# Moving 51 loads of a transformer block from SyncE's queue to GpSimd's

## The chip, the cores and the metric

The kernel runs on one core of a Trainium2 chip. The metric is the device time of one execution in microseconds (us); lower is better.

## The reference

One block of a diffusion transformer on x of 2048 tokens by 512 channels in bfloat16: six modulation vectors from c, a layer norm with scale and shift, attention in which each token sees eight keys at distances 0, 2, ..., 14 (32 heads of 16), an output projection with a gate, a second layer norm, and a gated feed-forward layer of width 1792.

```python
mod = (silu(c) @ w_mod).reshape(1, 6, 1, -1)
sa, ca, ga, sb, cb, gb = (mod[:, i] for i in range(6))
h = layernorm(x) * (1 + ca) + sa
q, k, v = split(h @ wqkv)                       # 32 heads of 16
idx = pos[:, None] - 2 * arange(8)[None, :]     # negative: masked
attn = softmax(einsum('bhsd,bhswd->bhsw', q, k[idx]) * 0.25)
x = x + ga * (einsum('bhsw,bhswd->bhsd', attn, v[idx]) @ wo)
h = layernorm(x) * (1 + cb) + sb
x = x + gb * ((silu(h @ w1) * (h @ w3)) @ w2)
```

## The kernel before

**Tiles.** The 2048 tokens are 16 tiles T of 128. `LN1` makes groups of tiles for the first layer norm and the projections to q, k and v; `BLOCKS` pairs of tiles for attention; `FFN` groups for the feed-forward layer.

**First layer norm.** For each pair of tiles VectorE takes mean and variance (L532, L533), GpSimd forms the reciprocal root in two small instructions (L537 adds epsilon, L539 takes the power), and VectorE normalizes (L544). TensorE transposes the result for the first tiles (L604), a DMA transpose does for the last four, and ScalarE applies scale and shift.

**Attention.** q and k stay transposed in SBUF. VectorE multiplies them for all eight distances (L706, "pq"), TensorE sums over heads (L716; for the first tile it also adds a mask, L712, that GpSimd makes in L399 and L400), then softmax. V is written to a scratch tensor in DRAM (`v_scratch_dram`) and read back in shifted rows, 768 KB for a tile (the V load, into two buffers `vsh0` and `vsh1` and, once the projection weights are dead, a third, `vshx`). VectorE multiplies by the weights of attention (L783), TensorE sums (L792), ScalarE copies out, a DMA transposes, TensorE multiplies by `wo` (L804), and VectorE adds to x (L808), whose sum gives the second mean.

**Second layer norm.** ScalarE takes squares (L558), GpSimd forms the reciprocal root (L564, L565), VectorE a bias (L566), ScalarE normalizes (L569). The result is transposed and goes to the feed-forward layer: `w1` and `w3` (L820), silu on ScalarE (L826), a product on VectorE (L831), `w2` (L863, L851), a final addition (L879) and the store.

**Loads.** `w1` and `w3` come in four column groups each (`w1_0` to `w3_3`), `w2` in four row groups (`w2_0` to `w2_3`); VectorE multiplies each `w2` group by the gate (L905) before its first use, and `wo` likewise (L896). The late modulation weights are `wm_g0`, `wm_g1` and `wm_s1`; a second load of x brings the rows of each tile in the order in which attention returns them, as four DMAs for four tiles. All DMAs are issued through `Program.dma` (L127).

**Order.** Every operation is recorded as an `Op` with an engine. The list `ORDER`, written out by hand or by a planner, gives one global order of all 1115 operations; `place` (L147) filters it into one queue for each engine, and `synchronize` (L169) finds the semaphore waits. An engine runs its queue strictly in this order, and an instruction that waits holds everything behind it in the same queue. `dma` has an argument `eng`, "sp" where nothing is said: it decides in whose queue the issuing instruction stands. Its waits stand there too:

```python
def section(e, todo=todo, eng=eng):
    for o in todo:
        for d in o.waits:
            e.wait_ge(d.inc[0], d.inc[2])
        ins = o.fn(e)
```

Before the change SyncE issues everything but the load of c: the loads, the stores of V and of the output, and all 32 DMA transposes. GpSimd runs only constants and the reciprocal roots.

Of the kernel before, what the change touches and what calls it, by code (L numbers as in the profile page):

```python
# [12 lines left out]
D = 512  # L13
H = 32
# [5 lines left out]
KT = D // P  # L20
# [219 lines left out]
def bass_adaLN_cond__sliding_local_dilated__glu_gated_swiglu__prompt_kernel(  # L240
    nc, A_x, A_wqkv, A_wo, B_x, B_w1, B_w3, B_w2, c, w_mod, out
):
    ctx = ExitStack()
    with ctx:
        p = Program(nc, ctx)
        _build(p, *[_full_ap(t) for t in (A_x, A_wqkv, A_wo, B_w1, B_w3, B_w2, c, w_mod, out)])
        p.place(ORDER, SLOTS)
        p.synchronize()
        p.emit()
# [11 lines left out]
def c_act(n):  # L261
    return 66 + n * 107 // 128


def c_dve(n):
    return 60 + n * 137 // 128
# [12 lines left out]
def _build(p, A_x, A_wqkv, A_wo, B_w1, B_w3, B_w2, c, w_mod, out):  # L279
# [6 lines left out]
    def sb(shape, dtype, name):  # L286
        return ctx.enter_context(nc.sbuf_tensor("sb_" + name, shape, dtype))
# [4 lines left out]
    w1 = sb([P, KT, F], bf, "w1")  # L292
    w3 = sb([P, KT, F], bf, "w3")
    w2 = sb([P, NF, D], bf, "w2")
# [38 lines left out]
    def at(shape, dtype, name, off):  # L333
        return nc.alloc_sbuf_tensor_at("sb_" + name, shape, dtype, offset=rbase + off)
# [3 lines left out]
    wm_s = [at([P, KT, 1024], bf, f"wm_s{i}", 12288 * i) for i in range(2)]  # L338
    zrow = at([PAD, D], bf, "zrow", 25600)
    thc, c4, c4s = at([KT, P], f32, "thc", 24576), at([KT, P], bf, "c4", 25088), at([KT, P], bf, "c4s", 25344)  # L340
    wm_g = [at([P, KT, 512], bf, f"wm_g{i}", 12288 * i + 8192) for i in range(2)]
# [6 lines left out]
    def bank(v):  # L348
        return PALL[:, v.at * 512:(v.at + 1) * 512]
# [52 lines left out]
    vkpad, vzrow, vvpad = Val("kpad"), Val("zrow"), Val("vpad")  # L402
# [3 lines left out]
    wm_view = w_mod.rearrange("(t p) n -> p t n", p=P)  # L406
    vcT = Val("cT")
    vx = [Val(f"x{T}") for T in range(NT)]
    vsx = [Val(f"sx{T}") for T in range(NT)]
    vwms, vwmg = [Val("wms0"), Val("wms1")], [Val("wmg0"), Val("wmg1")]  # L410
# [10 lines left out]
    for i in range(3):  # L421
        for half in range(2):
            p.dma(wqkv[:, half::2, i * D:(i + 1) * D], wqkv_view[:, half::2, i * D:(i + 1) * D], ("load", 3 + i), (256, 1024),
                  w=[vwq[i][half]])
    for g in range(1, 4):
        p.dma(x_sb[:, 4 * g:4 * g + 4, :], x_view[:, 4 * g:4 * g + 4, :], ("load", 5 + g), (512, 1024), w=vx[4 * g:4 * g + 4])
    late = {}
    late["wmg0"] = p.dma(wm_g[0][:], wm_view[:, :, 1024:1536], ("load", 9), (512, 1024), w=[vwmg[0]])
    vwo = Val("wo")
    for dl in range(4):  # L430
        late[f"wo{dl}"] = p.dma(wo[32 * dl:32 * dl + 32, :, :],
              bass.AP(A_wo.tensor, A_wo.offset + dl * D, [[16 * D, H], [4 * D, KT], [1, D]]), ("load", 10), (256, 1024), part=[vwo])
    p.dma(v_dram[0:PAD, :], zrow[:], ("load", 11), (16, 1024), r=[vzrow] + wm_hold, w=[vvpad], store=True)
    late["wms1"] = p.dma(wm_s[1][:], wm_view[:, :, 1536:2560], ("load", 12), (512, 2048), w=[vwms[1]])
    late["wmg1"] = p.dma(wm_g[1][:], wm_view[:, :, 2560:3072], ("load", 13), (512, 1024), w=[vwmg[1]])
    w1_view = B_w1.rearrange("(t p) n -> p t n", p=P)
    w3_view = B_w3.rearrange("(t p) n -> p t n", p=P)
    NG = 4
    cuts = [0, 4, 8, 11, 14]
    vw1, vw3, vw2 = [[Val(f"{m}_{g}") for g in range(NG)] for m in ("w1", "w3", "w2")]  # L440
    for g in range(NG):
        a, b = cuts[g] * P, cuts[g + 1] * P
        late[f"w1_{g}"] = p.dma(w1[:, :, a:b], w1_view[:, :, a:b], ("load", 14 + 2 * g), (512, 2 * (b - a)), w=[vw1[g]])
        late[f"w3_{g}"] = p.dma(w3[:, :, a:b], w3_view[:, :, a:b], ("load", 15 + 2 * g), (512, 2 * (b - a)), w=[vw3[g]])
    group_of = [next(g for g in range(NG) if fi < cuts[g + 1]) for fi in range(NF)]
    w2_view = B_w2.rearrange("(t p) n -> p t n", p=P)
    for g in range(NG):
        a, b = cuts[g], cuts[g + 1]
        late[f"w2_{g}"] = p.dma(w2[:, a:b, :], w2_view[:, a:b, :], ("load", 22 + g), (128 * (b - a), 1024), w=[vw2[g]])

    vthc, vcs = Val("thc"), Val("cs")
    k = ("mod", 0)
# [3 lines left out]
         r=[vthc, vcT], w=[vc4])  # L456
# [3 lines left out]
         r=[vc4, vident] + wm_hold, w=[vpc])  # L460
# [169 lines left out]
    vq, vk, vv_dram = {}, {}, {}  # L630
# [142 lines left out]
    def values(T, i, val):  # L773

        vv = Val("vsh", vshpool)
        p.dma(lambda: vv.at[:], bass.AP(v_dram, (PAD + T * P - 2) * D, [[4 * D, 32], [-4 * D, 4], [1, 6 * D]]), ("vl", T), (128, 6144),
              r=[vv_dram[T]] + ([] if T % 2 else [vv_dram[T - 1]] if T else [vvpad]), w=[vv], cost=640, again=True)
        vr = Val("pr", pqpool)

        def av(e):  # L780
            a_w = bass.AP(val.at, i * 8 * H, [[2 * 8 * H, P], [H, 8], [0, DH], [1, H]])
            v_w = bass.AP(vv.at, 2 * D, [[6 * D, P], [-2 * D, 2], [D, 4], [1, D]])
            return e.tensor_tensor(bass.AP(vr.at, 0, [[8 * D, P], [1, 8 * D]]), v_w, a_w, ALU.mult)  # L783

        avs[T] = p.op("dve", av, C_PQ, ("av", T), r=[val, vv], w=[vr], lock=True)
        vo, vt = Val("ps_o", psum), Val("ot", otpool)

        def acc(e):
            b = bank(vo)
            for wf in range(2):  # L790
                for c in range(4):
                    ins = e.matmul(b[32 * c:32 * c + 32, :], ind[:], bass.AP(vr.at, (4 * wf + c) * D, [[8 * D, P], [1, D]]),  # L792
                                   start=(wf == 0), stop=(wf == 1), tile_position=(0, 32 * c))
            return ins

        p.op("pe", acc, C_RED, ("ac", T), r=[vr, vind], w=[vo], tiled=True)
        va = Val("oa", oapool)
        p.op("act", lambda e: e.activation(va.at[:], bank(vo), ACT.Copy), c_act(512), ("ac", T), r=[vo], w=[va])
        p.dma(lambda: vt.at[:], lambda: va.at[:], ("ac", T), (128, 1024), r=[va], w=[vt], cost=1250, transpose=True)
        vy = Val("ps_y", psum)  # L800

        def wop(e):
            for ft in range(KT):
                ins = e.matmul(bank(vy), vt.at[:, ft, :], wo[:, ft, :], start=(ft == 0), stop=(ft == KT - 1))  # L804
            return ins

        p.op("pe", wop, 4 * MM, ("wo", T), r=[vt, vsc_wo], w=[vy])
        p.op("dve", lambda e: e.scalar_tensor_tensor(x_sb[:, T, :], bank(vy), 1.0, x_sb[:, T, :], op0=ALU.mult, op1=ALU.add,  # L808
                                                     accum_out=sx[:, T, :]), c_dve(512) + 12, ("rs", T), r=[vy], w=[vx[T], vsx[T]])
# [90 lines left out]
    for g in range(NG):  # L900
# [3 lines left out]
        a, b = cuts[g], cuts[g + 1]  # L904
# [3 lines left out]
    for T in range(0, NT, 4):  # L908
        loads = []
        for c in range(4):  # L910
            p.dma(x_sb[32 * c:32 * c + 32, T:T + 4, :], bass.AP(x2d.tensor, x2d.offset + (T * P + c) * D, [[4 * D, 32], [P * D, 4], [1, D]]),
                  ("xr", T), (128, 1024), part=vx[T:T + 4], group=loads)
    for groups in BLOCKS:
        vls = [logits(Ts) for Ts in groups]
        ves = [shift(Ts, vl) for Ts, vl in zip(groups, vls)]
        for Ts, vl, ve, vx_ in zip(groups, vls, ves, exps(groups, vls, ves)):
            val = softmax(Ts, vl, ve, vx_)
            for i, T in enumerate(Ts):
                values(T, i, val)
# [102 lines left out]
```

## Time and profile before

| | us |
|---|---|
| median of the two runs | 246.49 |
| the two runs | 245.53 and 247.45 |
| the profiled execution | 247.83 |
| its span, first to last instruction | 245.8 |
| TensorE busy | 234.7 (96%) |
| VectorE busy | 173.1 (70%) |
| ScalarE busy | 154.5 (63%) |
| GpSimd busy | 20.9 (8%) |

The span leaves out some 2 us of the execution's own time. A line of the timeline gives the start and the duration of an instruction (or of several in a row), its engine, its line in the kernel and what it writes and reads; in brackets stands the idle time before it and what ended it. "SPq" and "POOLq" are instructions in the queue of SyncE or GpSimd that issue DMAs. PE is TensorE, DVE VectorE, ACT ScalarE, POOL GpSimd.

### The profile page before, as it was taken

The page shows a single profiled execution, that of the slowest core. Times are in us where ns is not written, and L with a number is a line of the kernel's source. Part 1 is how long each engine was busy: PE and PEld are TensorE (multiplying, and loading weights), DVE is VectorE, ACT ScalarE, POOL GpSimd, SP SyncE. Part 2 cuts the span into 40 slices and gives each one's busy share as a digit, 9 for nine tenths or more (in the row PEclk, how much of TensorE's full clock was granted, in tenths as well). Part 3 has the DMA queues.
Part 4 walks back from the last instruction along what each step waited for, and adds up shares of the span by engine and source line. Part 5 has one row for each costly group of instructions (what it writes and reads, how often), then busy time and mean ns, then how long its engine had stood idle before and what let it go on. Part 6 is the DMA issues. An engine that isn't in the chain of part 4 may idle for free.

```text
span 245.8 us, 4285 instructions
## 1 busy us (share of the span) xinstructions
PE 234.7 (96%) x1669; PEld 120.1 (49%) x1669; DVE 173.1 (70%) x305; ACT 154.5 (63%) x305; POOL 20.9 (8%) x52
## 2 busy tenths in 40 slices
PE   7799999999998999899899999999999999999994
PEld 2557555444556666545443434443334444444473
DVE  4567999999897899988999996592942322142621
ACT  2168677797998889764587879456556944351200
POOL 4124111002000200031000001100000110000000
PEclk9799999999999999999999999999999999999999
DMA  6999979879958687703332964443031120010002
GB/s 191 345 311 350 303 273 207 188 185 350 299 131 249 217 214 244 173 21 67 87 126 59 266 164 154 72 109 121 21 87 23 43 65 16 9 57 9 3 19 67
DMA packets 39348, 36.21 MB, mean 147 GB/s; under 512 B 18832, under 2 KB 36256, under 8 KB 39328
## 3 DMA queue, kind: packets, MB, share of 16 engines
q1 hardware_dynamic: 39320, 35.94, 51.6%
q8 instruction: 13, 0.21, 0.4%
q14 instruction: 7, 0.06, 0.1%
q10 hardware_dynamic: 8, 0.00, 0.0%
HBM read 27.53 MB, written 4.21 MB: 129 GB/s over the span
## 4 chain that ended last, share of the span: by engine, by line
PE 48%; DMA 3%; ACT 2%; DVE 0%; issue 0%; DVEq 0%
PE pall L820 30%; PE pall L863 12%; PE pall L804 3%; DMA sb_h<-sb_xn 2%; PE pall L792 2%; DMA out_dram<-sb_o 1%; ACT sb_h L589 1%; PE pall L851 1%; DVE sb_o L879 0%; ACT sb_xn L569 0%; PE pall L716 0%; ACT sb_hh L830 0%; DVEq L225 0%
## 5 line engine op out<-in xcount | busy, mean ns | idle before, releaser
L820 PE MATMUL pall<-sb_h,sb_w 128*128 128x512 bf16 (+1 forms) x560 | 101.5, 337 | 1.4 <-ACT sb_h L589 1.0
L820 PEld LDWEIGHTS pall<-sb_h,sb_w 128*128 128x128 bf16 x560 | 51.5, 98 | 50.4 <-ACT sb_sg L826 5.8
L826 ACT ACTIVATE sb_sg<-pall 128x512 bf16<-128x512 f32 (+1 forms) x70 | 34.0, 514 | 26.5 <-PE pall L820 25.9
L863 PE MATMUL pall<-sb_w,sb_hh 128*128 128x512 bf16 x196 | 43.5, 379 | 0.0
L706 DVE TENSOR_TENSOR sb_pq<-sb_q,sb_kT 128x4096 bf16<-128x4096 bf16 x16 | 36.3, 2282 | 0.0
L656 PE MATMUL pall<-sb_h,sb_wqkv 128*128 128x512 bf16 (+1 forms) x160 | 33.0, 350 | 1.0 <-DVE sb_h L619 0.6
L830 ACT ACTIVATE sb_hh<-pall 128x256 bf16<-128x256 f32 (+1 forms) x56 | 26.3, 493 | 9.6 <-PE pall L820 9.0
L863 PEld LDWEIGHTS pall<-sb_w,sb_hh 128*128 128x128 bf16 x196 | 19.0, 98 | 22.8 <-DVE sb_hh L831 0.3
L783 DVE TENSOR_TENSOR sb_pq<-sb_vsh,sb_al 128x4096 bf16<-128x4096 bf16 x12 | 27.3, 2286 | 1.1 <-PE pall L716 0.8
L831 DVE TENSOR_TENSOR sb_hh<-sb_sg,sb_hh 128x256 bf16<-128x256 bf16 (+1 forms) x56 | 18.5, 352 | 11.7 <-ACT sb_hh L830 11.3
L879 DVE TENSOR_TENSOR sb_o<-pall,sb_x 128x512 bf16<-128x512 f32 (+1 forms) x18 | 11.0, 628 | 16.8 <-PE pall L863 12.4
L656 PEld LDWEIGHTS pall<-sb_h,sb_wqkv 128*128 128x128 bf16 x160 | 15.0, 102 | 15.2 <-ACT sb_v L685 1.2
L834 DVE TENSOR_TENSOR sb_hh<-sb_sg,pall 128x512 bf16<-128x512 bf16 x14 | 8.9, 684 | 15.3 <-PE pall L820 13.2
L804 PE MATMUL pall<-sb_wo,sb_ot 128*128 128x512 bf16 x64 | 16.0, 379 | 2.6 <-DMA sb_ot<-sb_oa 2.5
L589 ACT ACTIVATE sb_h<-sb_h,sb_modc 128x512 bf16<-128x512 bf16 x16 | 11.7, 811 | 10.0 <-DMA sb_h<-sb_xn 10.0
L612 ACT ACTIVATE sb_h<-pall,sb_modc 128x256 bf16<-128x256 bf16 (+1 forms) x22 | 12.5, 649 | 8.4 <-DVE sb_modc L487 6.1
L564 POOL TENSOR_SCALAR sb_rs<-sb_var 128x2 f32<-128x2 f32 x8 | 4.0, 500 | 147.7 <-ACT sb_xn L558 147.7
L675 PE MATMUL pall<-sb_wqkv,sb_h 128*128 128x512 bf16 x64 | 16.5, 379 | 0.0
L808 DVE SCALAR_TENSOR_TENSOR sb_x<-pall,sb_x 128x512 bf16<-128x512 f32 x16 | 10.9, 688 | 8.0 <-PE pall L804 7.9
L569 ACT ACTIVATE sb_xn<-sb_x,sb_nb,sb_rs 128x512 bf16<-128x512 bf16 x16 | 12.5, 809 | 4.4 <-DVE sb_nb L566 4.4
L665 ACT ACTIVATE sb_kT<-pall 128x512 bf16<-128x512 f32 (+1 forms) x20 | 9.9, 521 | 4.9 <-PE pall L656 4.7
L558 ACT ACTIVATE sb_xn<-sb_x,sb_nm 128x512 bf16<-128x512 bf16 x16 | 11.4, 713 | 2.3 <-DVE sb_nm L554 2.2
(79 smaller groups left out, 217.1 us busy)
## 6 DMA issues: line engine op xcount, KB each, us to landing
sb_vsh<-v_scratch_dram SPq DMA_DIRECT2D x12, 768.0 KB, 5.2
sb_w<-in_B_w_dram SPq DMA_DIRECT2D x6, 512.0 KB, 6.7
sb_vshx<-v_scratch_dram SPq DMA_DIRECT2D x4, 768.0 KB, 5.2
sb_x<-in_A_x_dram SPq DMA_DIRECT2D x18, 128.0 KB, 5.1
sb_w<-in_B_w_dram SPq DMA_DIRECT2D x6, 384.0 KB, 8.2
v_scratch_dram<-sb_v SPq DMA_DIRECT2D x16, 128.0 KB, 5.6
out_dram<-sb_o SPq DMA_DIRECT2D x14, 128.0 KB
sb_wqkv<-in_A_wqkv_dram SPq DMA_DIRECT2D x6, 256.0 KB, 6.4
```

The lines of the kernel that those rows point to most:

```text
L569: p.op("act", lambda e, vn=vn, T=T: e.activation(vn.at[:], x_sb[:, T, :], ACT.Identity, bias=nb[:, T, :], scale=rs[:, NT + T, :]), c_act(5 ...
L589: return e.activation(vh.at[:, ft, 0:n * P], vh.at[:, ft, 0:n * P], ACT.Identity, bias=modc[:, 8 * which + ft:8 * which + ft + 1], scale=m ...
L656: ins = e.matmul(bank(vp)[:, 0:n], wqkv[:, t, kind * D + ft * P:kind * D + (ft + 1) * P], vh.at[:, t, 0:n], start=(t == ORDER[0]), stop=(t ...
L675: ins = e.matmul(bank(vp), vh.at[:, t, tt * P:(tt + 1) * P], wqkv[:, t, 2 * D:3 * D], start=(t == ORDER[0]), stop=(t == ORDER[-1]))
L706: return e.tensor_tensor(vp.at[:], in0, in1, ALU.mult)
L783: return e.tensor_tensor(bass.AP(vr.at, 0, [[8 * D, P], [1, 8 * D]]), v_w, a_w, ALU.mult)
L804: ins = e.matmul(bank(vy), vt.at[:, ft, :], wo[:, ft, :], start=(ft == 0), stop=(ft == KT - 1))
L820: ins = e.matmul(bank(vp)[:, 0:n], wt[:, t, fi * P:(fi + 1) * P], vh.at[:, t, 0:n], start=(t == 0), stop=(t == KT - 1))
L826: p.op("act", lambda e: e.activation(vt.at[:, 0:n], bank(vgp)[:, 0:n], ACT.Silu), c_act(n), k, r=[vgp], w=[vt], table="silu")
L830: p.op("act", lambda e: e.activation(vh_.at[:, 0:n], bank(vup)[:, 0:n], ACT.Copy), c_act(n), k, r=[vup], w=[vh_])
L831: p.op("dve", lambda e: e.tensor_tensor(vh_.at[:, 0:n], vt.at[:, 0:n], vh_.at[:, 0:n], ALU.mult), 60 + n * 69 // 128, k, r=[vt], w=[vh_], ...
L863: ins = e.matmul(bank(vz), vhh[fi].at[:, tt * P:(tt + 1) * P], w2[:, fi, :], start=(fi == 0), stop=(fi == NF - 1))
```

## The change

51 DMAs get `eng="pool"` and keep their places in `ORDER`: the 16 V loads, the 16 DMAs of the second load of x, the 4 of `wo`, the 3 of the late modulation weights, and the 12 of `w1`, `w3` and `w2`. Their instructions, and the waits in front of them, now stand in GpSimd's queue between its reciprocal roots. SyncE keeps the first load of x, `wm_s0`, `wqkv`, the stores of V and of the output, and the transposes. No other instruction changes its engine, and the order on TensorE, VectorE and ScalarE is the same.

```diff
-    late["wmg0"] = p.dma(wm_g[0][:], ..., ("load", 9), (512, 1024), w=[vwmg[0]])
+    late["wmg0"] = p.dma(wm_g[0][:], ..., ("load", 9), (512, 1024), w=[vwmg[0]], eng="pool")
...
-              bass.AP(A_wo.tensor, ...), ("load", 10), (256, 1024), part=[vwo])
+              bass.AP(A_wo.tensor, ...), ("load", 10), (256, 1024), part=[vwo], eng="pool")
...
-    late["wms1"] = p.dma(wm_s[1][:], ..., ("load", 12), (512, 2048), w=[vwms[1]])
-    late["wmg1"] = p.dma(wm_g[1][:], ..., ("load", 13), (512, 1024), w=[vwmg[1]])
+    late["wms1"] = p.dma(wm_s[1][:], ..., ("load", 12), (512, 2048), w=[vwms[1]], eng="pool")
+    late["wmg1"] = p.dma(wm_g[1][:], ..., ("load", 13), (512, 1024), w=[vwmg[1]], eng="pool")
...
-        late[f"w1_{g}"] = p.dma(w1[:, :, a:b], ..., w=[vw1[g]])
-        late[f"w3_{g}"] = p.dma(w3[:, :, a:b], ..., w=[vw3[g]])
+        late[f"w1_{g}"] = p.dma(w1[:, :, a:b], ..., w=[vw1[g]], eng="pool")
+        late[f"w3_{g}"] = p.dma(w3[:, :, a:b], ..., w=[vw3[g]], eng="pool")
...
-        late[f"w2_{g}"] = p.dma(w2[:, a:b, :], ..., w=[vw2[g]])
+        late[f"w2_{g}"] = p.dma(w2[:, a:b, :], ..., w=[vw2[g]], eng="pool")
...
         p.dma(lambda: vv.at[:], bass.AP(v_dram, ...), ("vl", T), (128, 6144),
-              r=[...], w=[vv], cost=640, again=True)
+              r=[...], w=[vv], cost=640, again=True, eng="pool")
...
-                  ("xr", T), (128, 1024), part=vx[T:T + 4], group=loads)
+                  ("xr", T), (128, 1024), part=vx[T:T + 4], group=loads, eng="pool")
```

The queue of GpSimd after the change, from the built instructions, in the three places of which the prediction speaks (reciprocal roots by their tiles, loads by their names):

```
... L537 and L539 of T 2,3 | wo | wm_g0 | L537, L539 of T 4,5 | L537 of T 6,7 |
wm_g1 | w1_3 | L539 of T 6,7 | w1_2 | L537 of T 8,9 | wm_s1 | wo | L539 of T 8,9 |
w3_2 | L537 of T 10,11 | x | L539 of T 10,11 | x | x | x | V load | L399 | L400 | V load | ...
... V load | w2_1 | x | L564, L565 (first pair) | V load | w1_0 | w3_1 | w3_3 | x | x | ...
... L564, L565 (second pair) | x | V load into vshx | w2_0 | x | V load | ...
```

More of the change, by code (lines that the diff above doesn't have):

```diff
@@ L427, in _build @@
     late = {}
-    late["wmg0"] = p.dma(wm_g[0][:], wm_view[:, :, 1024:1536], ("load", 9), (512, 1024), w=[vwmg[0]])
+    late["wmg0"] = p.dma(wm_g[0][:], wm_view[:, :, 1024:1536], ("load", 9), (512, 1024), w=[vwmg[0]], eng="pool")
     vwo = Val("wo")
@@ L431, in _build @@
         late[f"wo{dl}"] = p.dma(wo[32 * dl:32 * dl + 32, :, :],
-              bass.AP(A_wo.tensor, A_wo.offset + dl * D, [[16 * D, H], [4 * D, KT], [1, D]]), ("load", 10), (256, 1024), part=[vwo])
+              bass.AP(A_wo.tensor, A_wo.offset + dl * D, [[16 * D, H], [4 * D, KT], [1, D]]), ("load", 10), (256, 1024), part=[vwo], eng="pool")
     p.dma(v_dram[0:PAD, :], zrow[:], ("load", 11), (16, 1024), r=[vzrow] + wm_hold, w=[vvpad], store=True)
-    late["wms1"] = p.dma(wm_s[1][:], wm_view[:, :, 1536:2560], ("load", 12), (512, 2048), w=[vwms[1]])
-    late["wmg1"] = p.dma(wm_g[1][:], wm_view[:, :, 2560:3072], ("load", 13), (512, 1024), w=[vwmg[1]])
+    late["wms1"] = p.dma(wm_s[1][:], wm_view[:, :, 1536:2560], ("load", 12), (512, 2048), w=[vwms[1]], eng="pool")
+    late["wmg1"] = p.dma(wm_g[1][:], wm_view[:, :, 2560:3072], ("load", 13), (512, 1024), w=[vwmg[1]], eng="pool")
     w1_view = B_w1.rearrange("(t p) n -> p t n", p=P)
@@ L442, in _build @@
         a, b = cuts[g] * P, cuts[g + 1] * P
-        late[f"w1_{g}"] = p.dma(w1[:, :, a:b], w1_view[:, :, a:b], ("load", 14 + 2 * g), (512, 2 * (b - a)), w=[vw1[g]])
-        late[f"w3_{g}"] = p.dma(w3[:, :, a:b], w3_view[:, :, a:b], ("load", 15 + 2 * g), (512, 2 * (b - a)), w=[vw3[g]])
+        late[f"w1_{g}"] = p.dma(w1[:, :, a:b], w1_view[:, :, a:b], ("load", 14 + 2 * g), (512, 2 * (b - a)), w=[vw1[g]], eng="pool")
+        late[f"w3_{g}"] = p.dma(w3[:, :, a:b], w3_view[:, :, a:b], ("load", 15 + 2 * g), (512, 2 * (b - a)), w=[vw3[g]], eng="pool")
     group_of = [next(g for g in range(NG) if fi < cuts[g + 1]) for fi in range(NF)]
@@ L448, in _build @@
         a, b = cuts[g], cuts[g + 1]
-        late[f"w2_{g}"] = p.dma(w2[:, a:b, :], w2_view[:, a:b, :], ("load", 22 + g), (128 * (b - a), 1024), w=[vw2[g]])
+        late[f"w2_{g}"] = p.dma(w2[:, a:b, :], w2_view[:, a:b, :], ("load", 22 + g), (128 * (b - a), 1024), w=[vw2[g]], eng="pool")
     vthc, vcs = Val("thc"), Val("cs")
@@ L776, in values @@
         p.dma(lambda: vv.at[:], bass.AP(v_dram, (PAD + T * P - 2) * D, [[4 * D, 32], [-4 * D, 4], [1, 6 * D]]), ("vl", T), (128, 6144),
-              r=[vv_dram[T]] + ([] if T % 2 else [vv_dram[T - 1]] if T else [vvpad]), w=[vv], cost=640, again=True)
+              r=[vv_dram[T]] + ([] if T % 2 else [vv_dram[T - 1]] if T else [vvpad]), w=[vv], cost=640, again=True, eng="pool")
         vr = Val("pr", pqpool)
```

## The prediction

> **What bounds the kernel now.** I read the head of the page first, then the busy time by stretches.
>
> ```profile
> span 245.8 us, 4285 instructions
> PE 234.7 (96%) x1669; PEld 120.1 (49%) x1669; DVE 173.1 (70%) x305; ACT 154.5 (63%) x305; POOL 20.9 (8%) x52
> ...
> core 0: us, PE busy (x) PEld busy (x) DVE busy (x) ACT busy (x) POOL busy (x), PEclk, DMA share, GB/s
> 19.00:62.00 43.00, 42.79 (x397) 22.58 (x395) 40.86 (x67) 33.83 (x66) 6.74 (x13) 1.00 0.93 266
> 62.00:112.00 50.00, 46.95 (x416) 30.42 (x415) 45.14 (x78) 42.16 (x99) 4.64 (x6) 1.00 0.66 189
> 112.00:206.00 94.00, 93.01 (x556) 39.90 (x555) 62.75 (x110) 63.54 (x112) 3.70 (x8) 1.00 0.36 94
> ```
>
> TensorE is busy nearly always, and from 19 to 112 us VectorE is too (40.86 of 43 and 45.14 of 50 us). Both run fixed queues. So there is no idle time in which a delay on either could be made good: what one of them waits before 112 us is added to the end, except for small gaps. From the other side there is little to win, 245.8 - 234.7 = 11 us of idle TensorE in all, part of it start and end.
>
> GpSimd is busy 8%, but the waits view shows what its queue is made of:
>
> ```profile
> POOL sb_rs L564 <- ACT sb_xn L558: 147.7, 8, 37.7
> POOL sb_rs L537 <- DVE sb_mv L533: 24.6, 7, 9.7
> ```
>
> It stands most of the time in front of a reciprocal root whose input is not there yet. Whatever is queued behind L564 waits with it. This is what the 51 moved loads meet, and it decides more than the work of issuing them.
>
> **The change, first place: issues between the first reciprocal roots (19 to 29 us).** Nothing in this trace is issued as a DMA by GpSimd, so its price c for one DMA is bounded by SyncE's rows, all from its timeline:
>
> ```profile
> 17.87 1.42 SPq L127 DMA_DIRECT2D sb_wm_s<-in_w_mod_dram  x1
> ...
> 23.62 0.43 SPq L127 DMA_DIRECT2D sb_x<-in_A_x_dram  x1
> ```
>
> 0.43 us is the least, 1.42 what an issue takes where a backlog holds it. Most of these loads have 512 rows and GpSimd's own instructions on 128 partitions take up to 0.86 (below), so I take c = 1.0, between the two. Now the roots, on GpSimd's timeline, and what VectorE does with the last of them:
>
> ```profile
> 18.72 0.22 POOL L537 TENSOR_SCALAR sb_rs<-sb_mv 128x2 f32<-128x2 f32 x1 [0.22 <-DVE sb_mv L533]
> 19.02 0.86 POOL L539 TENSOR_TENSOR sb_rs<-sb_rs,sb_cst 128x2 f32<-128x2 f32 x1
> 20.90 0.22 POOL L537 TENSOR_SCALAR sb_rs<-sb_mv 128x2 f32<-128x2 f32 x1 [1.02 <-DVE sb_mv L533]
> 21.20 0.71 POOL L539 TENSOR_TENSOR sb_rs<-sb_rs,sb_cst 128x2 f32<-128x2 f32 x1
> ...
> 24.18 0.71 POOL L539 TENSOR_TENSOR sb_rs<-sb_rs,sb_cst 128x2 f32<-128x2 f32 x1
> ...
> 26.04 0.72 DVE L544 TENSOR_SCALAR sb_xn<-sb_x,sb_mv,sb_rs 128x512 bf16<-128x512 bf16 x2
> ...
> 26.76 6.68 DVE L706 TENSOR_TENSOR sb_pq<-sb_q,sb_kT 128x4096 bf16<-128x4096 bf16 x3
> ...
> 33.20 0.28 PE L712 MATMUL pall<-sb_before,sb_ones 128*32 128x256 bf16 x1
> ```
>
> Between the L537 that ends at 18.94 (tiles 6, 7) and the end of the L539 for tiles 10, 11 stand seven moved DMAs: wm_g1, w1_3, w1_2, wm_s1, a quarter of wo, w3_2, a quarter of x. The roots left in that stretch take 0.86 + 0.22 + 0.71 + 0.22 + 0.71 = 2.7. The last ends at 18.9 + 2.7 + 7c = 21.7 + 7c instead of 24.9. VectorE uses it at 26.04 and is then full (L706 follows at once), so it is late by 7c - 4.3: **2.7 us** at c = 1.0, nothing at 0.43, 5.6 at 1.42. The other loads of this stage are needed much later or covered: wm_g1 is used by TensorE just ahead of the transposes of tile 8, which are late by then; the mask of L399 and L400, now behind four DMAs more, is ready some 0.8 us of its own work after 21.7 + 11c, at 33.5, and L712 wants it at 33.2 plus the shift of 2.7.
>
> **Second place: w1_0 behind the first L564.** SyncE issued the V load of tile 3 at 53.47 and w1_0 at 54.76, the first of three; behind each stands its landing, from a tile view of that one DMA. GpSimd's queue has the pair L564, L565 ahead of both:
>
> ```profile
> 53.47 0.62 SPq L127 DMA_DIRECT2D sb_vsh<-v_scratch_dram  x1
> ...
> DMA to landing us min/median/max: 8.5/8.5/8.5
> ...
> 54.76 3.41 SPq L127 DMA_DIRECT2D sb_w<-in_B_w_dram  x3
> ...
> DMA to landing us min/median/max: 9.0/9.0/9.0
> ...
> 57.95 0.71 POOL L565 TENSOR_TENSOR sb_rs<-sb_rs,sb_cst 128x2 f32<-128x2 f32 x1
> ...
> 62.76 2.28 DVE L783 TENSOR_TENSOR sb_pq<-sb_vsh,sb_al 128x4096 bf16<-128x4096 bf16 x1
> ...
> 64.59 0.60 PE L820 MATMUL pall<-sb_h,sb_w 128*128 128x256 bf16 x4
> ...
> sb_vsh<-v_scratch_dram SPq DMA_DIRECT2D x12, 768.0 KB, 5.2
> ```
>
> w1_0 landed at 54.8 + 9.0 = 63.8, 1.8 after the V load, and the first L820 started on it at 64.59; the V load landed at 62.0 and L783 started at 62.76. Both had under a microsecond to spare. After the change the V load starts at 58.66. With the median V load's 5.2 and c - 0.43 of dearer issue it lands at 64.4 (1.7 late for L783), and w1_0, 1.8 behind it, at 66.3: TensorE's first L820 is **1.7 us** late (1.1 at c = 0.43, 2.1 at 1.42). The two are one shift: L783 and L820 wait for the same queue, and each engine's later work hangs on the other.
>
> **Third place: w2_0 behind the second L564.** The same, with the V load into vshx and w2_0:
>
> ```profile
> 76.64 0.53 SPq L127 DMA_DIRECT2D sb_vshx<-v_scratch_dram  x1
> ...
> DMA to landing us min/median/max: 5.7/5.7/5.7
> ...
> 77.22 0.61 SPq L127 DMA_DIRECT2D sb_w<-in_B_w_dram  x1
> ...
> DMA to landing us min/median/max: 6.5/6.5/6.5
> ...
> 82.15 0.71 POOL L565 TENSOR_TENSOR sb_rs<-sb_rs,sb_cst 128x2 f32<-128x2 f32 x1
> ...
> 87.18 1.22 DVE L905 TENSOR_TENSOR sb_w<-sb_w,sb_gb_bc 128x2048 bf16<-128x2048 bf16 x1
> ...
> 90.31 1.22 DVE L905 TENSOR_TENSOR sb_w<-sb_w,sb_gb_bc 128x2048 bf16<-128x2048 bf16 x1
> ...
> 91.72 0.59 PE L863 MATMUL pall<-sb_w,sb_hh 128*128 128x512 bf16 x2
> ```
>
> Before, w2_0 landed at 83.7, 1.4 after vshx, with 3.5 us to spare for the L905 at 87.18. Now the pair ends at 82.86, a quarter of x takes c, vshx starts at 82.86 + c and lands 5.2 + c - 0.43 later, w2_0 another 1.4 behind: 91.0 at c = 1.0. L905 is 3.9 us late, and behind it on VectorE stand the products L831 and the second L905, which ends at 91.53, only 0.2 before TensorE's L863 needs it. So **3.7 us** reach TensorE (2.5 at c = 0.43, 4.5 at 1.42).
>
> **What is hidden.** After 112 us no load is late: VectorE is busy 62.75 of 94 us, V loads were issued as soon as a buffer came free, and behind the third to eighth L564 stand no more loads of w. One V load there now follows a pair L564, L565 that it preceded; its cover is the buffer that came free long before its use, and without that it would cost the pair and one issue, 0.9 + 1.0 = 2 us. On SyncE the stores and transposes lose the loads ahead of them; I book nothing for that and make it a rival.
>
> **The sum**: 2.7 + 1.7 + 3.7 = 8.1 us. On the profiled execution's 247.83 that is **255.9**; the two runs have their median at 246.49, 1.3 lower, and 8.1 more would be 254.6 there. At the ends: 0 + 1.1 + 2.5 = 3.6 gives 251.4, and 5.6 + 2.1 + 4.5 = 12.2 gives 260.0.
>
> By the Trainium skill (DMA: Bandwidth & Descriptors, Specifications) the first byte of a DMA issued by GpSimd comes at about 1 us against 0.6 for SyncE; an estimate from it, c = 0.43 + 0.4, would make the sum 1.5 + 1.5 + 3.3 = 6.3 and the time 254.1. No trace here shows it yet.
>
> **The rivals.**
>
> *VectorE holds GpSimd's issues up.* L544 on VectorE is the kind of instruction that falls between the issues of the first place:
>
> ```profile
> L544 DVE TENSOR_SCALAR sb_xn<-sb_x,sb_mv,sb_rs 128x512 bf16<-128x512 bf16 x12 | 4.5, 395 | 1.2 <-PE pall L604 1.1
> ```
>
> If each of the six of tiles 6 to 11 blocks GpSimd for its 0.395 us, 2.4 us are added: 258.3. For it: those L544 stand exactly there. Against: L537 and L539 next to L544 take 0.22 and 0.71, no more than elsewhere. The Trainium skill has such a rule (SBUF — State Buffer, Who interferes with whom): a VectorE copy or tensor_scalar in a two-port mode locks GpSimd out of SBUF, descriptor writes included, while tensor_tensor has no such mode. By that rule this rival has 0.1.
>
> *A dear issue.* If a load of 512 rows costs GpSimd far more than any SyncE issue, c = 2, the first place gives 9.7, the second 2.7, the third 5.7: 18.1 more, 265.9. For it: these loads have four times the rows of the others. Against: no row here is so long without a backlog. 0.17.
>
> *A cheap issue.* c = 0.43, the order alone counts: 251.4. 0.18.
>
> *Not slower: two queues instead of one.* All loads, stores and transposes ran in one queue (q1 carries 51.6% of the engines' span), and TensorE waited for transposes behind V loads:
>
> ```profile
> q1 hardware_dynamic: 39320, 35.94, 51.6%
> ...
> 74.46 1.02 PE L804 MATMUL pall<-sb_wo,sb_ot 128*128 128x512 bf16 x4 [1.30 <-DMA sb_ot<-sb_oa]
> 103.76 1.02 PE L804 MATMUL pall<-sb_wo,sb_ot 128*128 128x512 bf16 x4 [0.71 <-DMA sb_ot<-sb_oa]
> 105.69 1.04 PE L804 MATMUL pall<-sb_wo,sb_ot 128*128 128x512 bf16 x4 [0.48 <-DMA sb_ot<-sb_oa]
> ...
> sb_w<-in_B_w_dram SPq DMA_DIRECT2D x6, 512.0 KB, 6.7
> ```
>
> If transposes in a queue of their own come at once, 1.30 + 0.71 + 0.48 = 2.5 us go: 245.3. It decides only if w1_0 and w2_0 still come in time, w2_0 within 87.18 - 82.86 - 2c = 2.3 us of its issue, where the median w load of this size takes 6.7. 0.1, with the case that the moved loads somehow keep their old times among it (247.8).
>
> **Chances and range.** The forecast 0.45, the cheap issue 0.18, the dear one 0.17, the lock 0.1, no loss 0.1. A measurement of this kernel can tell about 2% from no change: below 241.6 is faster, above 251.4 slower. Faster needs more than the rival's whole gain: 0.03. Within 2% is the rest of that rival, 0.07, and somewhat under half of the cheap issue, which sits on the border, 0.08: 0.15. Slower: 0.82. The range is 249.5 to 266: from just under the cheap end to the dear one.
>
> **What would show it.** In the new profile GpSimd's L539 for tiles 10, 11 ends near 28.7 instead of 24.9, and VectorE idles before L544 on "POOL sb_rs L539". The first L820 starts 4.4 us later than 64.6, after an idle on a DMA into sb_w; the first L905 8.3 later than 87.2, and TensorE idles some 4 us before its first L863. After that everything keeps its old distances. If L820 and L863 do not wait for DMAs, the order on GpSimd does not matter and I am wrong; if DMA issues in GpSimd's queue are far from 1 us apart, c is wrong; if TensorE's waits lie after 112 us, I have missed a load.

## The result, and the profile after

The changed kernel takes 273.41 us (median of 272.34 and 274.48) against 246.49 before: a ratio of 1.109 with an interval of 1.083 to 1.136. The prediction said 255.9 us and a range of 249.5 to 266. The direction was right; the size was not, and 273.4 lies outside the range. Here and below times are medians of all executions of a kernel, and ratios leave out those over 1.5% longer than its fastest, which are the profiled ones of e2, e4 and e6 (255.74, 254.01 and 277.48 us), so that the lengths of waits read there hold for these executions.

The head of the page of the changed kernel:

```profile
span 270.6 us, 4284 instructions
PE 239.8 (89%) x1669; PEld 121.4 (45%) x1669; DVE 174.0 (64%) x305; ACT 155.0 (57%) x305; POOL 52.5 (19%) x103
...
PEclk9999999968999995999995999999999999999999
...
q0 software_dynamic: 5360, 22.81, 27.8%
q1 hardware_dynamic: 26472, 13.13, 21.8%
```

The span grew by 24.8 us, TensorE's busy time by 5.1 (234.7 before), so TensorE stood idle 19.7 us more. What moved is visible in the queues: q0, GpSimd's, carries 22.81 MB, and q1, which had 35.94 MB before, has 13.13 left. GpSimd is far from full.

The waits view of the changed kernel, first TensorE's rows (what waited, for what, us in total, times, longest), then VectorE's:

```profile
PE pall L804 <- DMA sb_ot<-sb_oa: 14.9, 4, 7.0
PE pall L820 <- ACT sb_h L589: 5.1, 1, 5.1
...
PE pall L820 <- DMA sb_w<-in_B_w_dram: 1.4, 1, 1.4
...
DVE sb_w L905 <- DMA sb_w<-in_B_w_dram: 4.5, 1, 4.5
...
DVE sb_xn L544 <- POOL sb_rs L539: 3.5, 3, 1.2
```

The last three rows are my three places: w1_0 late by 1.4 us, w2_0 late by 4.5, the reciprocal roots late for VectorE. The first two are not. L804 multiplies by wo what a **DMA transpose** delivers, and L589 is ScalarE working on another transpose's result. In the kernel before the same waits of TensorE had 2.5 and 1.0 us in all (the 2.5 are in its row of L804 further down):

```profile
PE pall L820 <- ACT sb_h L589: 1.0, 1, 1.0
```

So 12.4 + 4.1 = 16.5 us of the loss are waits for transposes, which SyncE issues before and after the change and which nobody touched.

Three clusters make them up. The first, with GpSimd's and SyncE's timeline of the changed kernel, and TensorE's row behind it:

```profile
47.52 0.57 POOL L127 DMA_DIRECT2D sb_vsh<-v_scratch_dram  x1 [5.83 <-DVE sb_pq L783]
48.08 0.77 POOL L127 DMA_DIRECT2D sb_w<-in_B_w_dram  x1
48.83 0.56 POOL L127 DMA_DIRECT2D sb_x<-in_A_x_dram  x1
...
48.70 2.62 SPq L127 DMA_TRANSPOSE sb_ot<-sb_oa  x2
...
57.07 1.46 PE L804 MATMUL pall<-sb_wo,sb_ot 128*128 128x512 bf16 x3 [5.06 <-DMA sb_ot<-sb_oa]
```

The same place on SyncE's timeline of the kernel before:

```profile
47.97 2.51 SPq L127 DMA_TRANSPOSE sb_ot<-sb_oa  x2
...
51.14 0.59 SPq L127 DMA_DIRECT2D sb_vsh<-v_scratch_dram  x1
51.78 0.59 SPq L127 DMA_DIRECT2D sb_w<-in_B_w_dram  x1
```

Before, the V load, w2_1 and x stood behind the two transposes in SyncE's queue. The transposes waited for ScalarE, so the loads waited too, though nothing of their own held them. In GpSimd's queue only their own semaphores hold them: they leave as soon as L783 frees the V buffer, 1.2 us ahead of the first transpose. The tile view of these two transposes, before and then after, gives the price:

```profile
DMA to landing us min/median/max: 2.3/2.3/2.4
```

```profile
DMA to landing us min/median/max: 7.4/7.9/8.3
```

The second cluster is at GpSimd's second pair L564, L565, which ends at 93.0 us and lets a quarter of x out at once. The timelines of GpSimd, SyncE, VectorE and TensorE of the changed kernel, and then the tile view of the transpose, before and after:

```profile
93.62 0.56 POOL L127 DMA_DIRECT2D sb_vshx<-v_scratch_dram  x1
94.16 0.78 POOL L127 DMA_DIRECT2D sb_w<-in_B_w_dram  x1
...
94.58 1.20 SPq L127 DMA_TRANSPOSE sb_ot<-sb_oa  x1
...
101.96 1.23 DVE L905 TENSOR_TENSOR sb_w<-sb_w,sb_gb_bc 128x2048 bf16<-128x2048 bf16 x1 [4.53 <-DMA sb_w<-in_B_w_dram]
...
103.92 0.59 PE L804 MATMUL pall<-sb_wo,sb_ot 128*128 128x512 bf16 x1 [6.95 <-DMA sb_ot<-sb_oa]
```

```profile
DMA to landing us min/median/max: 2.4/2.4/2.4
```

```profile
DMA to landing us min/median/max: 9.2/9.2/9.2
```

w2_0 is late for L905, as predicted. But TensorE does not get that far: it stands 6.95 us in front of L804, because the transpose left SyncE just behind x, vshx and w2_0. The third cluster is at 130 us: two quarters of x, a V load and another quarter of x leave GpSimd between 129.4 and 131.7, two transposes into sb_h leave SyncE at 130.9 and 132.2 and take 7.4 and 8.0 us (2.3 and 3.9 before), and the first L820 behind them waits 5.1 us. From 148 us on almost nothing is added.

The rest is TensorE itself. After each gap of 5 us or more the PEclk row drops (6, 8, 5, 5), and the mean of one L804, the matmul that stands behind two of these gaps, goes up. Its rows of the groups view, before and then after:

```profile
L804 PE MATMUL pall<-sb_wo,sb_ot 128*128 128x512 bf16 x64 | 16.0, 379 | 2.6 <-DMA sb_ot<-sb_oa 2.5
```

```profile
L804 PE MATMUL pall<-sb_wo,sb_ot 128*128 128x512 bf16 x64 | 18.5, 426 | 14.9 <-DMA sb_ot<-sb_oa 14.9
```

The windows view puts a price on it. In the changed kernel the granted clock is 0.50 from 55.85 to 62.68, from 100.22 to 107.05 and from 141.18 to 148.01 us, and TensorE works 13.6 us in these stretches; in the kernel before it is 0.50 only from 9.60 to 13.01, with 3.1 us of work (in both, besides, behind the last matmuls). Half of the difference is 5.2 us, an estimate of what the low clock adds, and TensorE's busy time grew by 5.1.

So the span's 24.8 us are: 16.5 waits for transposes, 5.1 more of busy time at a lower clock, 1.4 for w1_0, and 1.8 of the first place and small changes.

### The profile page after: what moved, and what is told of

It is laid out like the page before. It is cut to its first block, busy times and chain, and to the rows that moved or that the text cites. A ratio compares the mean times of both kernels' runs of the same rounds, so it can differ in the third digit from the quotient of the medians.

```text
span 270.6 us, 4284 instructions
## 1 busy us (share of the span) xinstructions
PE 239.8 (89%) x1669; PEld 121.4 (45%) x1669; DVE 174.0 (64%) x305; ACT 155.0 (57%) x305; POOL 52.5 (19%) x103
## 3 DMA queue, kind: packets, MB, share of 16 engines
q0 software_dynamic: 5360, 22.81, 27.8%
q1 hardware_dynamic: 26472, 13.13, 21.8%
## 4 chain that ended last, share of the span: by engine, by line
PE 44%; DMA 4%; ACT 2%; DVE 0%; issue 0%; DVEq 0%
PE pall L820 28%; PE pall L863 11%; DMA sb_h<-sb_xn 3%; PE pall L804 3%; PE pall L792 1%; DMA out_dram<-sb_o 1%; ACT sb_h L589 1%; PE pall L851 1%; DVE sb_o L879 0%; ACT sb_xn L569 0%; ACT sb_sg L826 0%; PE pall L716 0%; ACT sb_hh L830 0%; DVEq L225 0%
## 5 line engine op out<-in xcount | busy, mean ns | idle before, releaser
L820 PE MATMUL pall<-sb_h,sb_w 128*128 128x512 bf16 (+1 forms) x560 | 104.5, 344 | 7.1 <-ACT sb_h L589 5.1
L820 PEld LDWEIGHTS pall<-sb_h,sb_w 128*128 128x128 bf16 x560 | 52.9, 100 | 58.3 <-ACT sb_h L589 5.8
L656 PE MATMUL pall<-sb_h,sb_wqkv 128*128 128x512 bf16 (+1 forms) x160 | 32.4, 345 | 1.1 <-DVE sb_h L619 0.6
L804 PE MATMUL pall<-sb_wo,sb_ot 128*128 128x512 bf16 x64 | 18.5, 426 | 14.9 <-DMA sb_ot<-sb_oa 14.9
L783 DVE TENSOR_TENSOR sb_pq<-sb_vsh,sb_al 128x4096 bf16<-128x4096 bf16 x12 | 27.3, 2285 | 2.6 <-DMA sb_vsh<-v_scratch_dram 1.4
L589 ACT ACTIVATE sb_h<-sb_h,sb_modc 128x512 bf16<-128x512 bf16 x16 | 11.7, 812 | 14.0 <-DMA sb_h<-sb_xn 14.0
L564 POOL TENSOR_SCALAR sb_rs<-sb_var 128x2 f32<-128x2 f32 x8 | 3.5, 440 | 81.1 <-ACT sb_xn L558 81.1
L804 PEld LDWEIGHTS pall<-sb_wo,sb_ot 128*128 128x128 bf16 x64 | 5.8, 105 | 24.7 <-issue 11.9
L675 PE MATMUL pall<-sb_wqkv,sb_h 128*128 128x512 bf16 x64 | 16.5, 379 | 0.0
L664 ACT ACTIVATE sb_q<-pall 128x512 bf16<-128x512 f32 (+1 forms) x20 | 9.7, 519 | 11.3 <-PE pall L656 11.2
```

What stands on the lines that cost most here:

```text
L589: return e.activation(vh.at[:, ft, 0:n * P], vh.at[:, ft, 0:n * P], ACT.Identity, bias=modc[:, 8 * which + ft:8 * which + ft + 1], scale=m ...
L656: ins = e.matmul(bank(vp)[:, 0:n], wqkv[:, t, kind * D + ft * P:kind * D + (ft + 1) * P], vh.at[:, t, 0:n], start=(t == ORDER[0]), stop=(t ...
L675: ins = e.matmul(bank(vp), vh.at[:, t, tt * P:(tt + 1) * P], wqkv[:, t, 2 * D:3 * D], start=(t == ORDER[0]), stop=(t == ORDER[-1]))
L820: ins = e.matmul(bank(vp)[:, 0:n], wt[:, t, fi * P:(fi + 1) * P], vh.at[:, t, 0:n], start=(t == 0), stop=(t == KT - 1))
```

## The experiments

Three theories went in. **Order of arrival**: a transpose waits in the DMA engines behind loads that were issued shortly before it, whoever issued them; GpSimd's queue does harm only because it lets the loads out ahead. **Software queue**: what GpSimd issues delays SyncE's transfers whenever both are in flight, in any order. **My prediction's**: only loads that stand behind L564 are late. Lines in the rows below are shifted by the edits (L804 is L811 in the first experiment, L809 in the second and third, L816 in the fourth). All times stand against the kernel before on the same chip, 244.9 to 245.3 us.

### e1: the loads stay on GpSimd, but behind the transposes

```diff
...
+            if o.transpose:
+                last = o
+            elif last and o.dma and o.eng == "pool":
+                o.deps[last] = True
```

> All 51 loads stay on GpSimd; each one that stands behind a DMA transpose in the global order now also waits until that transpose has landed. Order-of-arrival theory (a transpose waits in the DMA engines for the loads that were issued shortly before it, from whichever queue): the waits of L804 on transposes (5.1 and 7.0 us) and of L820 at 138 us (5.1, before 1.0) go, and with them their cold clock; left are 1.0 us early, 1.4 at w1_0 and 3 to 4 at w2_0: 251 to 256 us. Software-queue theory (packets from GpSimd's queue hold up SyncE's whenever both are in flight, in any order): V loads and w loads still run beside most transposes, so most of it stays: over 265 us. My prediction's theory (only loads late behind L564 cost): the added waits can only make loads later: 273 us or more.

Measured: 257.56 us, ratio 1.049 (1.042 to 1.056). Of the loss more than half is gone, and yet the time lies 1.6 us above what order of arrival gave. TensorE's waits for transposes; GpSimd's and SyncE's timeline behind the second pair, which ends at 87.0 us; and the tile view of that transpose:

```profile
PE pall L811 <- DMA sb_ot<-sb_oa: 7.9, 4, 5.1
```

```profile
87.58 0.56 POOL L128 DMA_DIRECT2D sb_vshx<-v_scratch_dram  x1
88.12 0.78 POOL L128 DMA_DIRECT2D sb_w<-in_B_w_dram  x1
...
88.54 1.20 SPq L128 DMA_TRANSPOSE sb_ot<-sb_oa  x1
```

```profile
DMA to landing us min/median/max: 7.0/7.0/7.0
```

The first and third clusters are gone (the transposes at 48.5 and 49.7 us land after 3.3 and 2.5 us). The second stayed: its three loads stand ahead of the transpose in the order, so the added wait does not hold them; it is L564 that makes them late enough to leave just in front of it. That is why 5.1 us remain at L811.

### e4: no DMA on GpSimd at all, one early group of loads moved ahead of the transposes

All DMAs on SyncE, as before the change; in `ORDER` a quarter of x, the V load of tile 2 and w2_1 (numbers 369, 422, 51) stand ahead of the first pair of transposes into sb_ot (405) instead of behind it.

> All loads on SyncE as before the change; only in the global order a quarter of x, the V load of tile 2 and w2_1 stand ahead of the first two transposes into sb_ot instead of behind them (first place of the loss). GpSimd issues nothing. Order of arrival: these transposes land 3 to 5 us later than at 50.3 and 51.6, L804 starts that much later, and the end moves by as much: 249 to 252 us. Software queue: no load is in it, no change within 1 us: 246 to 247 us. My prediction's theory: no change either.

Measured: 251.58 us, ratio 1.022 (1.014 to 1.030), inside what order of arrival gave. SyncE's and TensorE's timeline, and the tile view of the two transposes:

```profile
47.18 0.59 SPq L127 DMA_DIRECT2D sb_vsh<-v_scratch_dram  x1
47.82 0.59 SPq L127 DMA_DIRECT2D sb_w<-in_B_w_dram  x1
48.45 3.03 SPq L127 DMA_TRANSPOSE sb_ot<-sb_oa  x2
...
54.92 1.46 PE L809 MATMUL pall<-sb_wo,sb_ot 128*128 128x512 bf16 x3 [4.20 <-DMA sb_ot<-sb_oa]
```

```profile
DMA to landing us min/median/max: 5.5/6.0/6.4
```

The first cluster appears without GpSimd's queue, from the order alone. The software queue theory gave 246 to 247 here and falls as the whole account. But the same two transposes take 1.9 us longer in the changed kernel (8.3 and 7.4 instead of 6.4 and 5.5), though the loads ahead of them are no larger there; that part the order does not explain, and the last section comes back to it.

### e6: my second and third place taken out, the transposes left

The changed kernel with the loads that stood behind the first two pairs L564, L565 put ahead of them, and no added wait:

```diff
+        for before, what in [(606, [429, 42, 45, 49]), (700, [377, 478, 50])]:
+            for n in what:
+                ORDER.remove(n)
+            at = ORDER.index(before)
+            ORDER[at:at] = what
```

> The changed kernel with only those seven loads ahead of the two pairs L564, L565, and nothing that waits for transposes: my prediction's second and third place are taken out and all the rest is left. My prediction's theory: 1.7 + 3.7 of its 8.1 us go, and as these were all of the loss that it knew behind the first roots, some 250 to 256 us remain. Order of arrival: the wait of 1.4 us for w1_0 goes, and the transpose at 94.6 us no longer finds x, vshx and w2_0 ahead of it, but the first cluster (5 us at L804, now with four more loads that may arrive ahead of its transposes) and the third (4 us at L820) stay: 260 to 270 us.

Measured: 273.4 us, ratio 1.112 (1.105 to 1.120): nothing is gained. Its profile has no wait for w1_0 on TensorE or for w2_0 on VectorE, and the time is the same. My prediction's theory (250 to 256) falls by this. Order of arrival had the sign, but it gave 260 to 270. TensorE's waits, GpSimd's and SyncE's timeline, and the tile view of the two transposes:

```profile
PE pall L809 <- DMA sb_ot<-sb_oa: 20.8, 5, 9.0
```

```profile
48.62 0.55 POOL L127 DMA_DIRECT2D sb_vsh<-v_scratch_dram  x1
49.16 2.24 POOL L127 DMA_DIRECT2D sb_w<-in_B_w_dram  x3
...
47.93 3.41 SPq L127 DMA_TRANSPOSE sb_ot<-sb_oa  x2
```

```profile
DMA to landing us min/median/max: 12.2/14.6/16.9
```

Four loads more now leave around the same two transposes, and these take 12.2 and 16.9 us instead of 8.3 and 7.4. I had allowed for four more loads ahead of the transposes, not for so long a delay. The four loads left after the first of the two (48.62 to 51.40 against 47.93), so this is not order of arrival alone: by the packet records in the last section they ran among the transposes' packets. And the three loads that were moved ahead of the second pair L564, L565 now leave at 85.17 to 87.03, just ahead of another pair of transposes, at 86.5 and 87.8, which take 9.6 and 8.7 us (4.0 and 3.3 in the kernel before).

### e5: both at once

The kernel of e1 with the moves of e6.

> All moved loads stay on GpSimd, and every one of them that the order has behind a transpose waits for that transpose to land; besides, the V load of tile 3, w1_0, w3_1 and w3_3 stand ahead of the first pair L564, L565 in the order, and a quarter of x, the V load of tile 6 and w2_0 ahead of the second. Order of arrival, with my two places L564 as the rest of the loss: the gap of 2.3 us before the first L820 and the one of 5.1 before L804 (the transpose that arrived just behind x, vshx and w2_0) both go; what is left is about 1 us of GpSimd's issuing between the first roots and 1 to 3 of small waits: 246 to 250 us on a chip where the kernel before takes 244.9. Software queue (a load issued by GpSimd delays SyncE's DMAs whenever both are in flight, or is slower by itself): moving three loads of x, V and w earlier changes only where they collide, and 254 us or more remain.

Measured: 250.82 us, ratio 1.022 (1.013 to 1.030), 0.8 us above what order of arrival gave and well below the 254 of the software queue. The transposes of the first and second cluster, in two tile views of this kernel:

```profile
DMA to landing us min/median/max: 2.4/2.5/2.6
...
DMA to landing us min/median/max: 2.3/2.3/2.3
```

All 51 loads are in GpSimd's queue, and these transposes take what they took before. Of the 27 us only some 5 are left: 2.3 of them are the first place (e7), the others small waits, such as 2.0 us at one L804 and 1.4 for w1_0, which now waits for a transpose ahead of it. By the ratios e5 gains 21 us on the changed kernel, e1 alone 15, e6 alone nothing: the two edits need each other, because a load that moves forward moves in front of a transpose.

### e2 and e3: the two halves of the change

Only the 16 V loads on GpSimd, and everything but them.

> Only the 16 V loads are issued by GpSimd, everything else as before the change. Order of arrival: each of the three places keeps one V load of 768 KB ahead of the transposes, at 250 to 300 KB per us some 2.5 to 3 us each, plus 1.7 us for the V load behind the first L564: 253 to 258 us. Software queue: V loads are the only traffic in it and have the largest packets (6144 bytes), so the transposes suffer nearly as in the full change: over 262 us. My prediction's theory: 1.7 us for the V load of tile 3 and nothing else: 248 to 249 us.

> All moved loads but the V loads are issued by GpSimd. Order of arrival: without the V loads' waits ahead of them in GpSimd's queue the loads of the first place (w2_1, x) leave some 5 us earlier and are gone when the first transposes into sb_ot come; w2_0, still behind the second L564, stands ahead of the transpose at 85 us with 512 KB (2 us); the third place has 256 KB of x (1 us); early roots 1 us, w1_0 0.5 to 1.5: 250 to 254 us. Software queue: 10 of the 23 MB stay in it, packets of 4096 bytes: 255 to 262 us. My prediction's theory: 1.0 + 1 + 2.5 = 4.5 us, 251 us.

Measured: 252.24 us, ratio 1.027 (1.020 to 1.034), for the V loads, and 255.59, 1.040 (1.033 to 1.047), for the others. Neither half is harmless, and each has transposes behind its loads. e2 lies 0.8 us below what order of arrival gave, far below the 262 of the software queue and above the 248 to 249 of my prediction's theory. TensorE's waits for transposes, first of e2, then of e3:

```profile
PE pall L804 <- DMA sb_ot<-sb_oa: 6.8, 3, 3.0
```

```profile
PE pall L804 <- DMA sb_ot<-sb_oa: 7.7, 2, 6.2
```

e3 is a miss for order of arrival, which gave 250 to 254; taken alone it would fit the software queue (255 to 262). Its timeline shows what I had left out. Without the V loads' waits in GpSimd's queue, w2_3 and w2_2 follow x and w2_0 at once:

```profile
84.06 0.78 POOL L127 DMA_DIRECT2D sb_w<-in_B_w_dram  x1
...
85.38 1.49 POOL L127 DMA_DIRECT2D sb_w<-in_B_w_dram  x2
...
85.03 1.22 SPq L127 DMA_TRANSPOSE sb_ot<-sb_oa  x1
```

That transpose took 8.1 us. The V loads' waits had held those weights back; taking them out of the queue put more bytes beside the transpose. Two of the weights left after it (85.38 to 86.87 against 85.03), and its 512 packets ran from 87.70 to 91.06 among GpSimd's; in the kernel before they ran within 0.6 us.

### e7, e8 and e9: the first place alone

GpSimd issues only the 18 loads that the order has in the first 35 us (e7). e8 is the kernel before, unchanged, for a profile on the same chip; e9 is e7 with six of the loads behind the root of tiles 10 and 11.

```diff
+        if eng == "pool" and len(self.ops) not in EARLY:
+            eng = "sp"
...
+        what = [48, 46, 40, 36, 47, 367]          # e9 only
+        for n in what:
+            ORDER.remove(n)
+        at = ORDER.index(246) + 1
+        ORDER[at:at] = what
```

> The first place alone: GpSimd issues only the 18 moved loads that the order has in the first 35 us (wm_g, wo, wm_s, w1_1, w1_2, w1_3, w3_0, w3_2, the first group of x, the V loads of tiles 0 and 1); SyncE issues all others, as before. My prediction's formula 7c - 4.3 gives 2.7 us at c = 1.0 and 0.7 at the 0.57 to 0.81 us that the trace of the changed kernel shows for one issue. Order of arrival has nothing to add but where the first transposes (tile 8, at 40 us) meet w3_0. So 245.5 to 247 us by the measured c, 247.5 or more by c = 1.0; the kernel before takes 244.9. If most of the loss stood here all the same, 250 or more.

> The kernel before, unchanged, on the chip of this set: its profile is the one that the next kernel's shifts are read against. Every theory expects the same time as the kernel before, within 0.5%.

> The 18 early loads stay on GpSimd, but six of them (w1_3, w1_2, wm_s1, a quarter of wo, w3_2, a quarter of x) stand behind the root of tiles 10 and 11 instead of between the roots. If issues between the roots make the first place, as my formula has it, then the L539 of tiles 10 and 11 ends at about 22 us, VectorE no longer waits for it, and the time is the one of the kernel before, ratio 0.995 to 1.004 where the 18 loads with the old order gave 1.0097. If GpSimd's issuing costs VectorE or the first loads time by itself (a port, slower transfers), the ratio stays at 1.007 or more.

Measured: e7 247.53 us, ratio 1.0097 (1.0063 to 1.0131), 2.3 us; e8 1.003 (1.000 to 1.006); e9 249.22, ratio 1.017 (1.014 to 1.020). e7 falls on the 2.7 of c = 1.0, not on the 0.7 of the measured c. VectorE's rows on its timeline, of e7 (L547 and L542 are L544 and L539):

```profile
19.91 0.81 DVE L547 TENSOR_SCALAR sb_xn<-sb_x,sb_mv,sb_rs 128x512 bf16<-128x512 bf16 x2 [1.14 <-POOL sb_rs L542]
...
23.27 0.41 DVE L547 TENSOR_SCALAR sb_xn<-sb_x,sb_mv,sb_rs 128x512 bf16<-128x512 bf16 x1 [1.24 <-POOL sb_rs L542]
```

It waits for two earlier roots, 1.14 and 1.24 us, and both add up; in e8 all its waits for roots come to 1.1 us, in e7 to 3.5. My formula looked only at the last root.

e9 is a miss, and an instructive one. The first part of its expectation came true, by the timelines of GpSimd and then VectorE:

```profile
22.39 0.71 POOL L547 TENSOR_TENSOR sb_rs<-sb_rs,sb_cst 128x2 f32<-128x2 f32 x1
...
42.87 2.29 DVE L791 TENSOR_TENSOR sb_pq<-sb_vsh,sb_al 128x4096 bf16<-128x4096 bf16 x1 [2.48 <-DMA sb_vsh<-v_scratch_dram]
```

The last root ends at 23.1 us, and VectorE gets through the norm without loss. But the six loads, issued 2.4 to 4.7 us later and in one row, now stand right in front of the V load of tile 1, which takes 13.0 us instead of 10.3 to land; L791 (L783 before) waits 2.5 us for it. These 2.5 of e9's 4.0 us fit order of arrival again, between loads; the rest I have not traced.

Taken together, order of arrival gave a range for each of e1 to e6 and hit one, e4: e1, e3, e5 and e6 lie 1.6, 1.6, 0.8 and 3.4 us above, e2 0.8 below. It says which transposes become late and which way an edit goes, and not how much. No experiment pointed to a version faster than the kernel before.

## Why the prediction was wrong, step by step

**The step that failed** is the sentence "On SyncE the stores and transposes lose the loads ahead of them; I book nothing for that and make it a rival". The transposes gain no free way; they get loads ahead of them, which until then SyncE's order had held behind. I saw the queue as a cost of issuing, and took away only its delays. It was also what kept bulk transfers behind the small ones that TensorE waits for. The rival "two queues instead of one" had the sign wrong: it expected transposes in a queue of their own to come at once, and to save 2.5 us; they cost 16.5. That this is the cause is shown by e1 (loads held, two clusters gone), e4 (a cluster made without GpSimd) and e5 (all clusters gone). How much of the delay comes from loads that leave just behind a transpose, through the other queue, is seen in packet records (below), but no run prices it by itself.

**First place.** Two errors that met. One issue on GpSimd measures 0.57 us for a load of 128 rows and 0.75 to 0.81 for 512 rows, not 1.0. (SyncE's rows in the kernel before, from which c was bounded, run wider than 0.43 to 1.42: from 0.33 for a store to 2.19 for a load of w in a backlog.)

```profile
24.31 0.81 POOL L127 DMA_DIRECT2D sb_w<-in_B_w_dram  x1
...
25.38 0.57 POOL L127 DMA_DIRECT2D sb_x<-in_A_x_dram  x1
25.98 0.74 POOL L539 TENSOR_TENSOR sb_rs<-sb_rs,sb_cst 128x2 f32<-128x2 f32 x1
```

In the changed kernel the root of tiles 10 and 11 ended at 26.7, not at 28.7. On the other side the slack of 4.3 us in "7c - 4.3" was not there, since earlier roots made VectorE wait too. The sum of 2.7 against 2.3 measured is right by accident.

**Second place.** "TensorE's first L820 is 1.7 us late": 1.40 by the row for sb_w above, and the mechanism is as described.

**Third place.** "L905 is 3.9 us late": 4.53. But that "3.7 us reach TensorE" did not come about: the wait for the transpose covers it. e6, with both places taken out and the time unchanged, does not price these two terms: the loads that it moves lengthen TensorE's waits for transposes (20.8 us at L804 instead of 14.9). With the loads held behind the transposes the same moves gain some 6.6 us by the ratios (e1 to e5), but there the wait of 5.1 us for a transpose goes with them.

**After 112 us.** "After 112 us no load is late" is true; the third cluster is a late transpose. The prediction named this sign ("if TensorE's waits lie after 112 us, I have missed a load"), and what it had missed was not a load.

**What was not booked at all**: the clock. The three long waits, 5.1 to 7.0 us, were each followed by 6.83 us at half clock; 16.5 us of waits brought 5.1 us of longer matmuls.

**The other rivals.** VectorE locking GpSimd out is not seen: issues between L544s take 0.57 to 0.81 us as elsewhere. A dear issue (c = 2) is out; the seven issues between the roots average 0.73 us, about as far from the cheap one (0.43) as from 1.0. The range ended at 266 because it was made from prices of c alone; no case in it let a transfer that was not moved become slower.

## What to carry to other kernels

A single in-order issue queue is also a priority: what stands behind a waiting transfer cannot overtake it into the DMA engines. Before moving loads to a second queue, list for each small transfer that the bottleneck waits for which loads the first queue held behind it, and ask when each would leave by its own semaphores alone; if that is just ahead of the small transfer, add at least what those bytes take, and expect some delay from those just behind it too. If the loads must go to another queue, give them a wait on that transfer, and then look what the wait holds up in turn.

## What the runs showed of the hardware

The transposes of the first two clusters, with 1.3 to 1.4 MB of loads issued in the 2 us ahead of them, take 7.4 to 9.2 us to land in the changed kernel, where the loads come through GpSimd's queue, and 5.5 and 6.4 us in e4, where they stand ahead in SyncE's own; without loads ahead they take 2.3 to 2.4.

Counted from the trace's packet records of the second cluster, the 512 packets of 256 bytes of that transpose, issued at 94.58 us, all ran between 99.46 and 102.16, 18 ns each at the median, and none in the 4.9 us before, while GpSimd's packets of 4096 and 6144 bytes (means of 196 and 418 ns) ran. In the kernel before the same 512 ran from 85.62 to 86.23. The two V loads that GpSimd issued from 96.33 on, after the transpose, did not get ahead of it: one of their packets ran at 101.6 us, all others from 102.3 on. So there it goes by arrival.

In e6 it does not. The 1024 packets of its two transposes, issued at 47.93 and 49.20 us, ran from 52.34 to 65.24, and the first landed only at 60.17. Among them, from 53.93 to 60.95, ran the 128 packets of 6144 bytes of a V load that GpSimd issued at 48.62, after the first of the two. A load that leaves behind a transpose costs it time too, then, when it comes through the other queue. That goes with the misses of order of arrival in e3 and e6, and may be the 1.9 us between e4 and the changed kernel.

The Trainium skill (DMA: Bandwidth & Descriptors, Queues, rings and completion order) says that each DMA engine takes turns between the queues that have work, packet by packet. The records of e6 look like that, with packets of both queues side by side for 7 us; those of the second cluster do not, where for 4.9 us one queue's packets ran alone. What inside the DMA engines makes the difference stays open; no run here looks there.

TensorE's granted clock falls after idle gaps. The clock row of e1's page (40 slices of 6.4 us):

```profile
PEclk9799999999799998999999999999999999999999
```

The 7 in the eleventh slice, 64.2 to 70.6 us, stands behind the gap of 2.28 us before its first L827, the 8 behind the one of 5.13. Between start and end of the profiles of this case, every gap of 2.28 us or more was followed by such a drop or lay in one (2.28 in e1, 2.98 and 3.03 in e2, 4.20 in e4, 5.06 to 6.95 in the changed kernel), and the shorter ones were not (2.17 in e3, 2.02 in e2, 2.01 in e5, 1.87 in e8). The length of the gap need not be all that counts. In the clock records of the changed kernel the drops begin at 55.85, 100.22 and 141.18 us, 13 and 12 times 3.41 us apart, and each lasts twice 3.41, so the clock seems to be set in steps of 3.41 us. Cut into such steps, e1's 2.28 us of idle time lie in one step and e3's 2.17 fall into two, 1.10 and 1.07; the longest idle time in one step without a drop behind it is the 2.02 of e2. By these runs, then, a step with 2.28 us of idle time lets the clock fall and one with 2.02 does not. The Trainium skill (TensorE: Matmul & The Clock Gate, Part 1: The HAM clock gate) puts the point at an idle window of about 3.4 us; here less idle time than that was enough, and the measurement decides.
